# Regrouping the up-projection, splitting the last evictions and exchanges at the seams, and moving the second layer's filter loads, in a two-layer spectral and MLP kernel

## The chip, the cores and the metric

The kernel runs on one core of one Trainium2 chip. The metric is the device time of one execution in microseconds (us). The "span" of a profile is the time from the first to the last instruction of that one profiled execution, about 1.8 us less than the device time. Engines: PE is TensorE, PEld its weight loads, DVE is VectorE, ACT is ScalarE, POOL is GpSimd, SP is SyncE.

## The reference

```python
def _A_ref(x, w_r, w_i):                       # spectral filter
    X = jnp.fft.rfft2(x.astype(jnp.float32), axes=(-2, -1))
    return jnp.fft.irfft2(X * (w_r + 1j * w_i), s=(S, D), axes=(-2, -1)).astype(jnp.bfloat16)

def _B_ref(x, w1, b1, w2, b2):                 # MLP
    y = _layernorm(x)
    h = _gelu(jnp.einsum("bsd,df->bsf", y, w1) + b1)
    return jnp.einsum("bsf,fd->bsd", h, w2) + b2

# S, D, F = 2048, 576, 4608; twice:
x = x + _A_ref(_layernorm(x), A_w_r, A_w_i)
x = x + _B_ref(_layernorm(x), B_w1, B_b1, B_w2, B_b2)
```

## The kernel before

x stays on the chip as 16 tiles of 128 rows. Per layer the stages are:

1. The spectral-in stage folds, transposes and transforms each tile along D, and begins the transform along S. Each tile's result goes through an "exchange", a DMA that spreads it over other partitions. In layer 1 this stage is woven into the down-projection of layer 0, and only the last tile's part is left over at the layer boundary.
2. The middle stage finishes the forward transform, multiplies by the filter, begins the inverse, and exchanges again.
3. The spectral-out stage finishes the inverse and adds.
4. The MLP runs in four passes of four tiles. Each pass has an up-projection (36 chunks of 128 hidden units, in 18 pairs) and a down-projection.

D = 576 is four and a half times 128. The half remainder of a pair of chunks is done by two 64-row matmuls that run side by side in the two halves of the array (in the trace they start 0.003 to 0.004 us apart). In the code, `full` is the 128-row part of a pair and `rest` the 64-row part.

```python
# up-projection: groups of three pairs, each in one of three two-bank PSUM buffers
for p in range(0, NFC // 2, 3):
    for k in range(2):
        acc[p + k] = big_ps([P, 2, 512])
        full(p + k, True)                  # 8 matmuls of 128 rows
    acc[p + 2] = big_ps([P, 2, 512])
    for k in range(3):
        rest(p + k, k == 2)                # 2 matmuls of 64 rows each
    gelu(p)
    gelu(p + 1)
    full(p + 2, False)
    gelu(p + 2)
    ...

# layer boundary: the last tile's spectral-in work, with filler matmuls on zeros
spec.fold(prev, nc.vector)
keep_busy(5)
spec.turn(prev)                            # PE transposes, one ACT copy
keep_busy(4)
spec.sqrt = True
spec.stats([prev])
spec.dft_d(prev)                           # 6 matmuls, one scaled ACT eviction
keep_busy(5)
spec.dft_v(prev, on_act=True)              # 4 matmuls, one ACT copy, one exchange

# end of the middle stage
if n == NT - 1:
    nc.vector.tensor_copy(out=h[:, 0], in_=ph[:, 0, 0:KP])
    ins = nc.scalar.copy(out=h[:, 1], in_=ph[:, 1, 0:KP]).ins
...
exchange(hx, E_ORDER[n], h)                # then keep_busy(20) opens the next stage

# after the MLP of layer 0: filter and inverse-matrix loads of layer 1
for j in range(4):
    b = ("y1", order[-1]) if j >= 2 else None   # groups 2, 3 behind the last copy
    load_w(j, 0, b); load_w(j, 1, b); load_i1(j, b)
```

Of the kernel before, what the change touches and what calls it, by code (L numbers as in the profile page):

```python
# [18 lines left out]
P = 128  # L19
# [104 lines left out]
def kernel(  # L124
# [82 lines left out]
    nc.vector.memset(c_eps[:, 1:2], EPS * EPS)  # L207
    marks = {}

    def keep_busy(n):  # L210
        pw = sm_ps([P, 512], F32)
        for _ in range(n):
            nc.tensor.matmul(pw[:], lhsT=zeros[:], rhs=zeros[:, 0:1].to_broadcast([P, 512]), start=True, stop=True)  # L213
# [87 lines left out]
    class SpectralIn:  # L301
# [4 lines left out]
        def fold(self, t, odd_engine):  # L306
# [2 lines left out]
            odd_engine.tensor_tensor(out=xf[:, DH:D], in0=x_sb[:, t, 0:DH], in1=x_sb[:, t, DH:D], op=ALU.subtract)  # L309
            self.st["xf", t] = xf  # L310

        def stats(self, tiles):
            for t, (_, rs) in zip(tiles, ln_scale(ln_bn(tiles), False, self.sqrt)):
                self.st["rs", t] = rs

        def turn(self, t):
            xf = self.st.pop(("xf", t))
            pt = sm_ps([P, 5, P])
            for ci, (start, _) in enumerate(CHUNKS):
                nc.tensor.transpose(pt[:, ci, :], xf[:, start : start + 128], ident[:])  # L320
            xT = work.tile([P, 5, P], BF16, tag="turn")
            marks["turn", t] = nc.scalar.copy(out=xT[:], in_=pt[:]).ins
            self.st["xT", t] = xT

        def fold_twice(self, t):
# [19 lines left out]
            nc.sync.dma_start_transpose(out=xT[:], in_=rows[:])  # L345
            self.st["xT2", t] = xT

        def dft_d(self, t):
            pz = big_ps([P, 2, 512])
            if ("xT2", t) in self.st:  # L350
                xT = self.st.pop(("xT2", t))
                for o in range(2):
                    at_rest = 4 * KH + o * KP
                    nc.tensor.matmul(pz[:, o, 0:KP], lhsT=xT[:, 4, :], rhs=c_fd2[:, at_rest : at_rest + KP], start=True, stop=False)
                    for part in range(2):
                        g = FOLDS.index((o, part))
                        nc.tensor.matmul(  # L357
                            pz[:, o, part * KH : (part + 1) * KH], lhsT=xT[:, g, :], rhs=c_fd2[:, g * KH : (g + 1) * KH],
                            start=False, stop=(part == 1),
                        )  # L360
            else:
                xT = self.st.pop(("xT", t))
                for o in range(2):
                    for q, ci in enumerate(HALF_CHUNKS[o]):
                        nc.tensor.matmul(
                            pz[:, o, 0:KP], lhsT=xT[:, ci, :], rhs=c_fd[:, 3 * o + q, :], start=(q == 0), stop=(q == 2),
                        )
            z = work.tile([P, 2, KP], BF16, tag="z", bufs=3)
            nc.scalar.activation(  # L369
                out=z[:].rearrange("p r (j o) -> p r o j", o=2),  # L370
                in_=pz[:, :, 0:KP].rearrange("p o (r j) -> p r o j", r=2),
                func=ACT.Copy, scale=self.st.pop(("rs", t)),
            )
            self.st["z", t] = z

        def dft_v(self, t, on_act):
            z = self.st.pop(("z", t))
            py = big_ps([P, 2, 512])
            for r, terms in enumerate((((0, 0), (2, 1)), ((0, 1), (1, 0)))):
                for q, (pl, ri) in enumerate(terms):  # L380
                    nc.tensor.matmul(  # L381
                        py[:, r, 0:KP], lhsT=c_k1[:, pl, :], rhs=z[:, ri], start=(q == 0), stop=(q == 1)
                    )
            y1 = work.tile([P, 2, KP], BF16, tag="y1", bufs=5)
            if on_act:
                ins = nc.scalar.copy(out=y1[:], in_=py[:, :, 0:KP]).ins  # L386
            else:
                ins = nc.vector.tensor_copy(out=y1[:], in_=py[:, :, 0:KP]).ins
            marks["y1", t] = ins
            exchange(self.vx, t, y1[:])  # L390

        def run_all(self, loads):
# [6 lines left out]

            for i in range(NT + 4):  # L400
                if 0 <= i - 1 < NT:
                    self.turn(order[i - 1])
                if i < NT:
                    self.fold(order[i], nc.vector)
                    if i == 0:
                        moments(0)
                if i % 2 == 1 and i < NT:
                    for tt, (_, rs) in zip(order[i - 1 : i + 1], ln_scale(pairs.pop(i // 2), False, self.sqrt)):
                        self.st["rs", tt] = rs
                if 0 <= i - 4 < NT:  # L410
                    self.dft_v(order[i - 4], on_act=(i % 2 == 0))
                if 0 <= i - 2 < NT:
                    self.dft_d(order[i - 2])
                if i < 4:
                    keep_busy((5, 1, 1, 1)[i])
                if i + 1 < NT:
                    moments(i + 1)
                for call in loads.get(i, ()):
                    call()

    exchanged = {}

    def exchange(dst, slot, src):
        p0 = 32 * (slot // 4) + slot % 4
        ins = nc.sync.dma_start(out=dst[p0 : p0 + 29 : 4], in_=src).ins
        before = exchanged.setdefault(id(dst), [])
        for b in before:
            tc.declare_no_dep(ins, b, query=mybir.DependencyQuery.ANY_SYNC, reason="other partitions of the array")
# [2 lines left out]
    def middle(vx, hx, wks, i1s, loads):  # L431
# [32 lines left out]
        def idft_c(n):  # L464
# [5 lines left out]
                    nc.tensor.matmul(ph[:, o, 0:KP], lhsT=i1[:, n % 4, pl, :], rhs=xp[:, ri, :], start=(q == 0), stop=(q == 1))  # L470
            h = at(r_sb, [P, 2, KP], 592 * (2 + 9 + n % 8))
            if n == NT - 1:
                nc.vector.tensor_copy(out=h[:, 0], in_=ph[:, 0, 0:KP])
                ins = nc.scalar.copy(out=h[:, 1], in_=ph[:, 1, 0:KP]).ins
            elif n % 8 == 2:
                ins = nc.vector.tensor_copy(out=h[:], in_=ph[:, :, 0:KP]).ins
            else:
                ins = nc.scalar.copy(out=h[:], in_=ph[:, :, 0:KP]).ins
            marks["h", n] = ins
            exchange(hx, E_ORDER[n], h)  # L480

        keep_busy(12)
        for i in range(NT + 4):
# [173 lines left out]
    def mlp_up(yT, loads=()):  # L657
        hts = []
        loads = list(loads)
        acc = {}  # L660

        def full(p, first):
            ph = acc[p]
            for q in range(2):
                fc = 2 * p + q
                for ci in range(4):
                    nc.tensor.matmul(  # L667
                        ph[:, q, :], lhsT=w1_sb[:, ci, fc * 128 : (fc + 1) * 128], rhs=yT[:, ci, :],
                        start=(first and ci == 0), stop=(not first and ci == 3),
                    )  # L670

        def rest(p, first):
            for q in range(2):
                rows = slice(64 * q, 64 * q + 64)
                nc.tensor.matmul(acc[p][:, q, :], lhsT=w1r_sb[rows, p, :], rhs=yT[rows, 4, :], start=first, stop=not first)  # L675

        def gelu(p):
            for q in range(2):
                fc = 2 * p + q
                ht = at(h_sb, [P, 512], 512 * fc)  # L680
                marks["ht", fc] = nc.scalar.activation(  # L681
                    out=ht[:], in_=acc[p][:, q, :], func=ACT.Gelu_apprx_tanh, bias=b1_sb[:, fc : fc + 1], scale=1.0
                ).ins
                hts.append(ht)

        for p in range(0, NFC // 2, 3):
            for k in range(2):
                acc[p + k] = big_ps([P, 2, 512])
                full(p + k, True)
            acc[p + 2] = big_ps([P, 2, 512])  # L690
            for k in range(3):
                rest(p + k, k == 2)
            gelu(p)
            gelu(p + 1)
            full(p + 2, False)
            gelu(p + 2)
            if loads:
                loads.pop(0)(("ht", 2 * p))
        return hts
# [1 line left out]
    def mlp_down(t, i, hts, store, between):  # L701
# [3 lines left out]
        po = big_ps([P, 2, 512])  # L705

        def step(fc, h):
            nc.tensor.matmul(  # L708
                po[:, h, 0:DH], lhsT=hts[fc][:, i * 128 : (i + 1) * 128], rhs=w2_chunk(fc)[:, h * DH : (h + 1) * DH],
                start=(fc == 0), stop=(fc == NFC - 1),  # L710
            )

        if store and t == order[-1]:
            for h in range(2):
                for fc in range(NFC):
                    step(fc, h)
                nc.vector.tensor_tensor(out=xr[:, h], in0=po[:, h, 0:DH], in1=xb[:, h], op=ALU.add)  # L717
                nc.sync.dma_start(out=ov[:, t, h * DH : (h + 1) * DH], in_=xr[:, h])
            return
        for fc in range(NFC):  # L720
            for h in range(2):
# [8 lines left out]
    def mlp(li, prep, spec, loads):  # L730
        past = []
        last = li == N_LAYERS - 1
        for q in range(4):
# [6 lines left out]
            for i, t in enumerate(QUADS[q]):  # L740
# [17 lines left out]
                if spec is not None and len(past) > 1:  # L758
                    p = past[-2]
                    k = 2 if t != order[-1] else 0  # L760
                    slots[k].append(lambda p=p: spec.dft_d(p))
                    slots[k + 2].append(lambda p=p: spec.dft_v(p, on_act=True))
                mlp_down(t, i, hts, last, slots)
                past.append(t)
        if spec is not None:
            prev = past[-1]
            spec.fold(prev, nc.vector)
            keep_busy(5)
            spec.turn(prev)
            keep_busy(4)  # L770
            spec.sqrt = True
            spec.stats([prev])
            spec.dft_d(prev)
            keep_busy(5)
            spec.dft_v(prev, on_act=True)

    first = [("x", 2), ("x", 3)]
    for j in range(4):
# [13 lines left out]
    for li in range(N_LAYERS):  # L792
# [3 lines left out]
        if li == 0:  # L796
# [6 lines left out]
                6: [lambda b: load(c_fd2[:], const_ap("fd2"), b)],  # L803
                5: [lambda b: load(b2_bc[:], B_b2.partition_broadcast(P), b)],
            }
        middle(vx, hx, wks, i1s, mid_loads)
        if li == 0:
            b1p = sm_ps([P, NFC])
# [10 lines left out]
        else:  # L819
            vx, hx = at(b_sb, [P, 16, 2, KP]), at(v_sb, [P, 16, 2, KP])  # L820
            mlp(li, prep, SpectralIn(vx, sqrt=False), w2_loads)
            for j in range(4):
                b = ("y1", order[-1]) if j >= 2 else None
                load_w(j, 0, b)
                load_w(j, 1, b)
                load_i1(j, b)

_INS = ['A_x', 'A_w_r', 'A_w_i', 'B_x', 'B_w1', 'B_b1', 'B_w2', 'B_b2']
_OUTS = [((1, 2048, 576), 'bfloat16')]
# [24 lines left out]
```

## Time and profile before

The time before is 753.89 us, the median of 4 runs (753.38 to 754.26). Stage lengths below are start-to-start distances of matmuls in the profile of that kernel:

| stage | us | what limits it |
|---|---|---|
| spectral-in, layer 0 | 42.81 | varies from run to run |
| middle, layer 0 | 28.53 | the last 6.05 us are an exchange with fillers |
| spectral-out, each | 26.13 | |
| MLP, layer 0 | 300.92 | PE |
| boundary: last down-projection matmul to the middle stage | 9.32 | chain over all engines |
| middle, layer 1 | 27.10 | the last 4.61 us are an exchange with fillers |
| MLP, layer 1 | 286.66 | PE |

The first two lines of the profile page before give the span and the busy times. PE is busy 97% of the span:

```profile
span 752.0 us, 12318 instructions
PE 728.6 (97%) x5009; PEld 450.4 (60%) x5009; DVE 274.3 (36%) x930; ACT 312.6 (42%) x527; POOL 60.7 (8%) x110
```

The next lines are from the timeline of PE before, in an up-projection. The columns are start, length from the first start to the last end, engine, line, operation, output and inputs, shape and count; idle time before the group comes last in brackets, if there is any.

```profile
608.52 0.82 PE L675 MATMUL psb<-yT,w1r_sb 64*128 64x512 bf16 x6
609.28 5.35 PE L667 MATMUL psb<-yT,w_sb 128*128 128x512 bf16 x24
614.57 0.82 PE L675 MATMUL psb<-yT,w1r_sb 64*128 64x512 bf16 x6
```

There is no idle bracket: PE looks fully busy. Still, the period of 6.04 us (608.525 to 614.565 in the unrounded trace) is more than its matmuls need. Inside a run of equal matmuls, starts are 0.216 us apart. At the change from 128 to 64 rows the distance is 0.312, at the change back 0.311, and the next one is 0.226. That is 0.20 us more per group than 27 steps of 0.216. Modelled ends hide such a loss, so it has to be read from the starts.

At the layer boundary, PE before (L213 are the fillers, L320 the transposes, L365 and L381 the transforms, L440 the middle stage):

```profile
399.51 0.66 PE L381 MATMUL psb<-z,c_k 128*128 128x290 bf16 x4
400.01 1.25 PE L213 MATMUL pss<-zeros 128*128 128x512 bf16 x5
401.10 0.44 PE L320 MATMUL pss<-ident,xf 128*128 128x128 bf16 x5
401.37 1.03 PE L213 MATMUL pss<-zeros 128*128 128x512 bf16 x4
402.32 0.92 PE L365 MATMUL psb<-c_fd,xT 128*128 128x290 bf16 x6
403.08 1.25 PE L213 MATMUL pss<-zeros 128*128 128x512 bf16 x5
404.24 0.66 PE L381 MATMUL psb<-z,c_k 128*128 128x290 bf16 x4
404.74 2.77 PE L213 MATMUL pss<-zeros 128*128 128x512 bf16 x12
408.71 2.65 PE L440 MATMUL psb<-b_sb,c_f 128*128 128x290 bf16 x20 [1.20 <-DMA b_sb<-y]
```

Every group of fillers ends about where the useful group behind it begins. The data come in step with them: the fold that the transposes read ends at 401.03 us, the copy behind them at 402.26 and the scaled eviction at 404.19, each 0.05 to 0.07 us before the group that uses it starts. The fold waits for VectorE's add of the last tile, which is one instruction over the whole tile before:

```profile
399.71 0.76 DVE L726 TENSOR_TENSOR x_sb<-psb,xb 128x576 bf16<-128x576 f32 x1 [5.83 <-PE psb L708]
```

The ends of the two middle stages before, PE (L213 again are fillers, L508 the stage behind):

```profile
66.62 4.53 PE L213 MATMUL pss<-zeros 128*128 128x512 bf16 x20
72.33 0.60 PE L508 MATMUL pss<-c_r,b_sb 128*128 128x256 bf16 x4 [1.19 <-DMA b_sb<-shared]
...
431.33 4.52 PE L213 MATMUL pss<-zeros 128*128 128x512 bf16 x20
435.81 0.60 PE L508 MATMUL pss<-c_r,v_sb 128*128 128x256 bf16 x4
```

In layer 0 PE waits 1.19 us for the exchange after its fillers have run out; in layer 1 the fillers end last. The last tile of the kernel has one plain wait, of the second half on the add of the first:

```profile
744.32 2.12 PE L708 MATMUL psb<-v_sb,h_sb 128*128 128x288 bf16 x16 [0.55 <-DVE x_sb L717]
```

### The profile page before, as it was taken

To read this page: it belongs to the slowest core of one execution; us is meant where nothing else is said; L and a number is where in the kernel's file an instruction comes from. 1 tells how busy PE (TensorE), PEld (TensorE's weight loads), DVE (VectorE), ACT (ScalarE), POOL (GpSimd) and SP (SyncE) were. 2 spreads that over 40 slices of the span, in tenths; PEclk is the share of its full clock that TensorE was granted. 3 is DMA by queue.
4 is the path that set the end of the run, shared out by engine and by line. 5 is a ranking of instruction groups with operands and counts; after the bars stand their busy time and mean duration, and the time that the engine had idled before them with its cause. 6 is when DMAs were issued, how large, how long until landed. Compare 5 with 4: busy or idle time off the path is not lost. (4 is left out here: it accounts for less than half of the span.)

```text
span 752.0 us, 12318 instructions
## 1 busy us (share of the span) xinstructions
PE 728.6 (97%) x5009; PEld 450.4 (60%) x5009; DVE 274.3 (36%) x930; ACT 312.6 (42%) x527; POOL 60.7 (8%) x110
## 2 busy tenths in 40 slices
PE   7879999999999999999998998999999999999998
PEld 4645744784478447844785565457546744774476
DVE  6765970366036603630353969002400140010011
ACT  7955865114621453145323776530262035105600
POOL 3220002000100100000022000200100010000000
PEclk9999999999999999999999999999999999999999
DMA  7844926210121012110035400640002010100000
GB/s 247 232 140 146 280 81 229 54 44 26 44 56 49 26 45 53 51 35 0 18 85 177 123 21 16 218 120 17 34 17 44 17 42 2 44 17 9 1 17 17
DMA packets 49417, 54.45 MB, mean 72 GB/s; under 512 B 29892, under 2 KB 41104, under 8 KB 49360
## 3 DMA queue, kind: packets, MB, share of 16 engines
q0 software_dynamic: 7600, 29.10, 12.3%
q1 hardware_dynamic: 41328, 23.99, 12.0%
q8 instruction: 39, 0.64, 0.4%
q10 hardware_dynamic: 432, 0.58, 0.2%
q14 instruction: 18, 0.15, 0.1%
HBM read 29.34 MB, written 8.59 MB: 50 GB/s over the span
## 5 line engine op out<-in xcount | busy, mean ns | idle before, releaser
L681 ACT ACTIVATE h_sb<-psb,b_sb 128x512 bf16<-128x512 f32 x288 | 171.6, 695 | 231.2 <-PE psb L675 231.2
L708 PEld LDWEIGHTS <-h_sb 128*128 128x128 bf16 x2304 | 224.9, 98 | 58.3 <-issue 0.7
L667 PE MATMUL psb<-yT,w_sb 128*128 128x512 bf16 x1152 | 258.3, 379 | 0.1
L667 PEld LDWEIGHTS <-w_sb 128*128 128x128 bf16 x1152 | 108.7, 98 | 143.9 <-issue 20.6
L708 PE MATMUL psb<-shared,h_sb 128*128 128x288 bf16 x1280 | 166.8, 286 | 0.0
L726 DVE TENSOR_TENSOR x_sb<-psb,xb 128x576 bf16<-128x576 f32 x31 | 23.5, 757 | 356.8 <-PE psb L708 356.8
L708 PE MATMUL psb<-v_sb,h_sb 128*128 128x288 bf16 x1024 | 131.2, 286 | 0.5 <-DVE x_sb L717 0.5
L369 ACT ACTIVATE z<-psb,rs 128x580 bf16<-128x580 f32 x32 | 29.5, 920 | 89.9 <-PE psb L357 79.7
L273 DVE BATCH_NORM_STATS2 stats<-x_sb 128x6 f32<-128x288 bf16 x112 | 44.6, 440 | 1.1 <-DMA x_sb<-in_A_x_dram 1.1
L675 PE MATMUL psb<-yT,w1r_sb 64*128 64x512 bf16 x288 | 39.4, 380 | 0.0
L386 ACT CAST y<-psb 128x580 bf16<-128x580 f32 x24 | 15.5, 645 | 37.9 <-PE psb L381 36.7
L213 PE MATMUL pss<-zeros 128*128 128x512 bf16 x110 | 29.4, 396 | 1.0 <-DVE h_sb L229 1.0
L632 DVE TENSOR_SCALAR xn<-x_sb,mv,rs 128x576 bf16<-128x576 bf16 x24 | 9.3, 426 | 57.3 <-DMA quad<-xn 56.9
L544 DVE TENSOR_TENSOR shared<-psb,x_sb 128x576 f32<-128x576 f32 x32 | 24.0, 751 | 16.3 <-PE psb L536 16.2
L536 PE MATMUL psb<-c_gd,u 128*128 128x288 bf16 x128 | 24.9, 286 | 2.6 <-DVE x_sb L550 1.9
L442 ACT CAST shared<-psb 128x580 bf16<-128x580 f32 x32 | 20.4, 642 | 15.1 <-PE psb L440 10.5
L513 ACT CAST u<-pss 128x512 bf16<-128x512 f32 x32 | 18.6, 581 | 17.7 <-PE pss L508 17.1
L675 PEld LDWEIGHTS <-w1r_sb 64*128 64x128 bf16 x288 | 10.2, 94 | 26.0 <-issue 20.3
L470 PE MATMUL psb<-shared,h_sb 128*128 128x290 bf16 x128 | 21.4, 285 | 2.7 <-DVE shared L458 1.3
L704 DVE TENSOR_TENSOR xb<-x_sb,b_bc 128x576 f32<-128x576 bf16 x32 | 23.9, 748 | 0.0
L343 POOL DMA_DIRECT2D rows<-xf x14 | 7.6, 540 | 194.6 <-DVE xf L335 194.6
L381 PE MATMUL psb<-z,c_k 128*128 128x290 bf16 x128 | 21.1, 286 | 0.6 <-ACT z L369 0.6
(99 smaller groups left out, 521.3 us busy)
## 6 DMA issues: line engine op xcount, KB each, us to landing
shared<-in_B_w_dram POOLq DMA_DIRECT2D x4, 1440.0 KB, 7.8
w_sb<-in_B_w_dram SPq DMA_DIRECT2D x16, 288.0 KB
v_sb<-in_B_w_dram POOLq DMA_DIRECT2D x4, 1152.0 KB, 6.2
quad<-xn POOLq DMA_DIRECT2D x24, 160.0 KB, 2.6
h_sb<-const_i POOLq DMA_DIRECT2D x8, 384.0 KB, 6.1
v_sb<-y SPq DMA_DIRECT2D x16, 145.0 KB
b_sb<-shared SPq DMA_DIRECT2D x16, 145.0 KB
b_sb<-y SPq DMA_DIRECT2D x16, 145.0 KB
```

The source lines that it names most:

```text
L213: nc.tensor.matmul(pw[:], lhsT=zeros[:], rhs=zeros[:, 0:1].to_broadcast([P, 512]), start=True, stop=True)
L273: nc.vector.bn_stats(out=stats[:, h, :], in_=x_sb[:, t, h * DH : (h + 1) * DH])
L369: nc.scalar.activation(out=z[:].rearrange("p r (j o) -> p r o j", o=2), in_=pz[:, :, 0:KP].rearrange("p o (r j) -> p r o j", r=2), func=AC ...
L470: nc.tensor.matmul(ph[:, o, 0:KP], lhsT=i1[:, n % 4, pl, :], rhs=xp[:, ri, :], start=(q == 0), stop=(q == 1))
L536: nc.tensor.matmul(po[:, o, 0:DH], lhsT=lhsT, rhs=c_gd[:, 3 * o + q, :], start=(q == 0), stop=(q == 2))
L544: nc.vector.tensor_tensor(out=tt, in0=po[:, 0:1, 0:DH].to_broadcast([P, 2, DH]), in1=xr, op=ALU.add)
L667: nc.tensor.matmul(ph[:, q, :], lhsT=w1_sb[:, ci, fc * 128 : (fc + 1) * 128], rhs=yT[:, ci, :], start=(first and ci == 0), stop=(not first ...
L675: nc.tensor.matmul(acc[p][:, q, :], lhsT=w1r_sb[rows, p, :], rhs=yT[rows, 4, :], start=first, stop=not first)
L681: marks["ht", fc] = nc.scalar.activation(out=ht[:], in_=acc[p][:, q, :], func=ACT.Gelu_apprx_tanh, bias=b1_sb[:, fc : fc + 1], scale=1.0).ins
L704: nc.vector.tensor_tensor(out=xb[:], in0=xr, in1=b2_bc[:].rearrange("p (h n) -> p h n", h=2), op=ALU.add)
L708: nc.tensor.matmul(po[:, h, 0:DH], lhsT=hts[fc][:, i * 128 : (i + 1) * 128], rhs=w2_chunk(fc)[:, h * DH : (h + 1) * DH], start=(fc == 0), ...
L726: nc.vector.tensor_tensor(out=xr, in0=po[:, :, 0:DH], in1=xb[:], op=ALU.add)
```

## The change

The intent is to shorten what PE waits for or wastes at the seams. It has six parts:

- up-projection groups of four pairs instead of three, the fourth in the two one-bank PSUM buffers;
- both halves of the last tile's down-projection independent of each other, in both layers, each half with its own add, and at the layer boundary the layer norm's statistics by halves too;
- the last tile's evictions split over ScalarE and VectorE, with fewer fillers at the boundary (4, 3, 3 for 5, 4, 5);
- the last exchange of each spectral-in and middle stage in two halves;
- the two last copies of the middle stage side by side;
- the layer-1 loads of groups 2 and 3 moved into the middle stage.

```diff
+    def apart(a, b):
+        tc.declare_no_dep(b, a, query=mybir.DependencyQuery.ANY_SYNC, reason="other bank, other half of the tile")
...                                                    # turn, last tile
-            marks["turn", t] = nc.scalar.copy(out=xT[:], in_=pt[:]).ins
+            n = 3 if halved else 5
+            marks["turn", t] = nc.scalar.copy(out=xT[:, 0:n], in_=pt[:, 0:n]).ins
+            if halved:
+                nc.vector.tensor_copy(out=xT[:, n:5], in_=pt[:, n:5])
...                                                    # dft_d, last tile
+            if halved:
+                za = nc.scalar.activation(out=to[:, :, 0], in_=frm[:, :, 0], func=ACT.Copy, scale=rs).ins
+                apart(za, nc.vector.tensor_scalar(out=to[:, :, 1], in0=frm[:, :, 1], scalar1=rs, scalar2=None, op0=ALU.mult).ins)
...                                                    # dft_v, last tile
+            if halved:
+                for r in range(2):
+                    was, ins = ins if r else None, (nc.scalar.copy, nc.vector.tensor_copy)[r](out=y1[:, r], in_=py[:, r, 0:KP]).ins
+                    if r:
+                        apart(was, ins)
+                    exchange(self.vx, t, y1, r)
...                                                    # end of the middle stage
-                nc.vector.tensor_copy(out=h[:, 0], in_=ph[:, 0, 0:KP])
+                ha = nc.vector.tensor_copy(out=h[:, 0], in_=ph[:, 0, 0:KP]).ins
                 ins = nc.scalar.copy(out=h[:, 1], in_=ph[:, 1, 0:KP]).ins
+                apart(ha, ins)
...
-            exchange(hx, E_ORDER[n], h)
+            for r in (0, 1) if n == NT - 1 else (None,):
+                exchange(hx, E_ORDER[n], h, r)
...                                                    # mlp_up
-        for p in range(0, NFC // 2, 3): ...
+        for p in range(0, NFC // 2, 4):
+            ahead = [p, p + 1] if p + 3 < NFC // 2 else [p]
+            behind = [a + len(ahead) for a in ahead]
+            for a in ahead:
+                place(a)                               # p % 4 == 3: two small buffers
+                full(a, True)
+            for a in behind:
+                place(a)
+            for a in ahead + behind:
+                rest(a, a in behind)
+            for a in ahead:
+                gelu(a)
+            for a in behind:
+                full(a, False)
+                gelu(a)
...                                                    # mlp_down, last tile of each layer
+            for n in range(2 * NFC):
+                h, fc = divmod(n, NFC)
+                ins = step(fc, h).ins
+                if h == 1:
+                    apart(added, ins)
+                ...
...                                                    # layer boundary
-            keep_busy(5)
-            spec.turn(prev)
-            keep_busy(4)
-            spec.sqrt = True
-            spec.stats([prev])
-            spec.dft_d(prev)
-            keep_busy(5)
-            spec.dft_v(prev, on_act=True)
+            spec.stats_half(prev, 1)
+            spec.stats_end(prev)
+            keep_busy(4)
+            spec.turn(prev, halved=True)
+            spec.scale(prev)
+            keep_busy(3)
+            spec.dft_d(prev, halved=True)
+            keep_busy(3)
+            spec.dft_v(prev, on_act=True, halved=True)
...                                                    # loads of layer 1
+        if li == 1:
+            mid_loads = {
+                0: [lambda b: load_w(2, 0, b), lambda b: load_w(2, 1, b)],
+                1: [lambda b: load_i1(2, b), lambda b: load_w(3, 0, b)],
+                2: [lambda b: load_w(3, 1, b), lambda b: load_i1(3, b)],
+            }
...
-            for j in range(4):
-                b = ("y1", order[-1]) if j >= 2 else None
+            for j in range(2):
```

## The prediction

> What bounds the kernel now. TensorE is busy 97% of the 752 us span at full granted clock (busy table, slices). The two MLP stages take about 588 us of it (98 to 399, 462 to 749); the group table gives the 512-column up-projection matmuls 0.1 us of idle in all. So time can come only from (a) TensorE's pace in the up-projection and (b) the seams where TensorE waits or runs filler: end of the first spectral stage (41 to 44 us), of the first middle stage (67 to 72), the layer boundary (399 to 409), the end of the second middle stage (431 to 436), the last tile (744).
>
> Costs, term by term.
>
> 1. Up-projection grouping. The timeline repeats every 6.04 us: 24 full matmuls, 6 half-height ones. Full ones start 0.216 us apart, half-height pairs 0.216; at the change of height the distance is 0.312 going in, 0.311 coming out, plus 0.01 on the next: 0.20 us lost per group. The Trainium skill, "TensorEngine Tiling (Array Packing)", Key Properties, says a change of tiling mode drains the engine; the trace agrees. Groups per pass fall from 6 to 5, in 8 passes: -1.6 us. ScalarE needs about 1.2 us per pair of GELUs, TensorE 1.9, so the new PSUM placement should not stall; w2 loads are triggered later but land several us before use.
>
> 2. Last tile. TensorE waits between the halves for VectorE's add (chain of waits; it resumes at 744.32 instead of about 743.60). Removed: -0.7 us.
>
> 3. Layer boundary, all on the critical path. Before: last matmul starts 399.39, fillers hold the transposes until 401.10, copy 0.69, matmuls, scaled eviction 0.92, matmuls, copy 0.64, exchange issued 405.60, next stage starts 408.71. After: one filler fewer before the transposes (-0.22), eviction of 3 of 5 chunks (about -0.2; both engines read one bank, so I expect them one after the other, still covered by the first matmuls), scaled eviction on two engines (-0.4), last copy split (-0.2). The exchange becomes two issues; SyncE spends 0.71 us per issue back to back, so the second starts about 404.98: perhaps 0.1 more. Sum -1.1 us (0.7 to 1.4).
>
> 4. First spectral stage. The two last copies wait for exchanges of earlier tiles (buffer release, 1.2 and 1.8 us in the waits); DMA moves a steady 180 GB/s there. The halved work upstream hides behind that: -0.15 us.
>
> 5. Middle ends. The serial pair of copies (ScalarE waits 0.78 us for VectorE) becomes parallel, but in layer 0 the last exchange is bound by queue drain: -0.1. In layer 1 the 20 fillers end just when the next stage starts (435.81): 0.
>
> 6. Loads of layer 1. Two groups start about 4 us later, within the last tile, the others move into the middle stage. They should land 1 us before use; DMA there gets busier: +0.1, with a tail of +1.
>
> Sum: about -3.6 us, 750.3 us; 748.7 to 752.0 holds it 8 times in 10. Faster by over 2%: 1%; within 2%: 98%; slower by over 2%: 1%.
>
> What would show it. Half-height batches of 8 and 4, a pass 0.2 us shorter; no wait on the add at 744; boundary (last down-projection matmul to first of the middle stage) 8.2 us instead of 9.3; second middle stage unchanged, 27.1 us.
>
> What would make it wrong. Half exchanges of 580-byte packets landing later than one whole one; VectorE's half copy waiting for the first half exchange; layer-1 weights late, or their traffic delaying the last exchange as in layer 0 (4.8 us from issue to use there, 3.4 in layer 1); GELU stalls.

## The result

After: 751.22 us, the median of 11 runs (749.47 to 753.39). Before, in the same rounds and the earlier ones: 754.2 us, the median of 16 (752.29 to 759.3). The ratio is 0.9955 with a 95% interval of 0.9938 to 0.9973. It is not quite the ratio of those medians. The profiled execution of the kernel after has a span of 748.4 us, with PE again busy 97%. 0.9955 of 754.2 us is 3.4 us less, where 3.6 were predicted.

The stages, before and after. "Other profiles" are the runs below whose code in that stage equals the one named (the last row leaves out runs with a whole exchange, which moves the end; see below):

| stage | before | other profiles of that code | after | other profiles of that code | predicted change |
|---|---|---|---|---|---|
| spectral-in 0 | 42.81 | 41.84 to 43.86 | 42.85 | 42.00 to 44.23 | -0.15 |
| middle 0 | 28.53 | 27.79, 27.88, 28.03 | 27.40 | 27.39, 27.40, 27.81, 28.36, and 28.86 with half clock | -0.1 |
| MLP 0 | 300.92 | 300.92 | 300.08 | 300.09 | -0.8 |
| boundary | 9.32 | 9.34, 9.38, 9.43 | 8.49 | 8.47 to 8.50 | -1.1 |
| middle 1 | 27.10 | 27.04, 27.13, 27.26 | 27.57 | 27.37, 27.39, 27.49 | +0.1 |
| MLP 1 with last tile | 286.66 | 286.66 | 285.12 | 285.11, 285.12 | -1.5 |
| last matmul's start to the end | 3.42 | 3.41 to 3.43 | 3.67 | 3.66 to 3.68 | 0 |

The MLP, the boundary and the last tile repeat. Spectral-in and the first middle stage move by a microsecond or more between runs of one and the same code, which hides any small gain there.

The up-projection after, PE timeline (L708 are the 128-row and L716 the 64-row matmuls):

```profile
605.82 0.82 PE L716 MATMUL psb<-yT,w1r_sb 64*128 64x512 bf16 x6
606.48 0.38 PE L716 MATMUL pss<-yT,w1r_sb 64*128 64x512 bf16 x2
606.79 1.90 PE L708 MATMUL psb<-yT,w_sb 128*128 128x512 bf16 x8
```

The batch now has 8 matmuls of 64 rows. The cost of one change of height is as before: 605.506 to 605.817 going in (0.311), 606.476 to 606.787 coming out (0.311). There are fewer of them. The pass, start to start, is 71.31 us instead of 71.52.

The boundary after, PE (L216 fillers, L336 transposes, L384 and L403 transforms, L473 middle stage):

```profile
397.58 0.66 PE L403 MATMUL psb<-z,c_k 128*128 128x290 bf16 x4
398.08 1.03 PE L216 MATMUL pss<-zeros 128*128 128x512 bf16 x4
398.95 0.44 PE L336 MATMUL pss<-ident,xf 128*128 128x128 bf16 x5
399.23 0.81 PE L216 MATMUL pss<-zeros 128*128 128x512 bf16 x3
399.96 0.92 PE L384 MATMUL psb<-c_fd,xT 128*128 128x290 bf16 x6
400.72 0.81 PE L216 MATMUL pss<-zeros 128*128 128x512 bf16 x3
401.56 0.66 PE L403 MATMUL psb<-z,c_k 128*128 128x290 bf16 x4
402.05 2.77 PE L216 MATMUL pss<-zeros 128*128 128x512 bf16 x12
405.95 2.64 PE L473 MATMUL psb<-b_sb,c_f 128*128 128x290 bf16 x20 [1.12 <-DMA b_sb<-y]
```

Row by row against before: to the transposes 1.37 us instead of 1.59, from there to the first transform 1.01 for 1.22, to the second 1.60 for 1.92, to the middle stage 4.39 for 4.47. The last step holds the last copy, which is faster (0.46 us for 0.64), and the exchange, which is not (3.27 us from its first issue to its use, for 3.11). The first step holds an edit that is easy to overlook: only the second half's add is left at the seam, 0.46 us for 0.76.

```profile
397.79 0.46 DVE L765 TENSOR_TENSOR x_sb<-psb,xb 128x288 bf16<-128x288 f32 x1 [4.70 <-PE psb L753]
```

So the fold ends 0.30 us earlier, counted from the matmuls of the first row, and that is what let a filler go: with the old add the fold ended only 0.07 us before the transposes.

VectorE's part of the transposes' copy, after, in VectorE's timeline:

```profile
399.94 0.29 DVE L341 COPY xT<-pss 128x256 bf16<-128x256 bf16 x1 [0.52 <-ACT xT L339]
```

It waits for ScalarE's part, as the prediction expected. The Trainium skill, "PSUM — Partial Sum Buffer", section "PSUM bank collisions raise a hardware error", says that two engines must not access one PSUM bank on the same partitions at the same time, reads included; here both halves lie in one bank and the framework puts them one after the other (0.52 us of wait). It costs nothing, because the first transform's matmuls start on ScalarE's part.

The ends of the two middle stages after, PE (L543 is the stage behind):

```profile
66.66 4.53 PE L216 MATMUL pss<-zeros 128*128 128x512 bf16 x20
71.24 0.60 PE L543 MATMUL pss<-c_r,b_sb 128*128 128x256 bf16 x4
...
428.55 4.52 PE L216 MATMUL pss<-zeros 128*128 128x512 bf16 x20
433.52 0.60 PE L543 MATMUL pss<-c_r,v_sb 128*128 128x256 bf16 x4 [0.46 <-DMA v_sb<-shared]
```

The two have changed places in these two profiles: in layer 0 the wait for the exchange is gone, in layer 1 there is a new one of 0.46 us.

The last tile after, PE:

```profile
738.03 2.61 PE L753 MATMUL psb<-shared,h_sb 128*128 128x288 bf16 x20
740.48 2.12 PE L753 MATMUL psb<-v_sb,h_sb 128*128 128x288 bf16 x16
```

The second half follows without a gap. The 0.25 us lost at the very end comes from the closing checks. SyncE checks its DMA semaphores one after the other, 0.062 us each. Before, the last store's semaphore was late in the list and three checks remained after it; after, it is early in the list and seven remain. The change only renumbered the semaphores. Two runs below with one issue less, e6 and e8, agree: there the last store comes still later in the list, one check remains after it, and the end takes 3.31 and 3.30 us.

### The profile page after: what moved, and what is told of

It is laid out like the page before. It is cut to its first block, busy times and chain, and to the rows that moved or that the text cites. A ratio compares the mean times of both kernels' runs of the same rounds, so it can differ in the third digit from the quotient of the medians.

```text
span 748.4 us, 12355 instructions
## 1 busy us (share of the span) xinstructions
PE 726.5 (97%) x5005; PEld 451.5 (60%) x5005; DVE 276.3 (37%) x936; ACT 315.4 (42%) x528; POOL 60.6 (8%) x110
## 5 line engine op out<-in xcount | busy, mean ns | idle before, releaser
L722 ACT ACTIVATE h_sb<-psb,b_sb 128x512 bf16<-128x512 f32 x224 | 138.1, 686 | 225.8 <-PE psb L716 217.8
L708 PE MATMUL psb<-yT,w_sb 128*128 128x512 bf16 x896 | 206.9, 379 | 0.1
L708 PEld LDWEIGHTS <-w_sb 128*128 128x128 bf16 x1152 | 109.4, 98 | 142.4 <-issue 17.2
L395 ACT ACTIVATE z<-psb,rs 128x580 bf16<-128x580 f32 x30 | 27.6, 921 | 88.6 <-PE psb L376 79.8
L708 PE MATMUL pss<-yT,w_sb 128*128 128x512 bf16 x256 | 60.5, 379 | 0.0
L722 ACT ACTIVATE h_sb<-pss,b_sb 128x512 bf16<-128x512 f32 x64 | 40.5, 690 | 0.0
L716 PE MATMUL psb<-yT,w1r_sb 64*128 64x512 bf16 x224 | 31.1, 380 | 0.0
L216 PE MATMUL pss<-zeros 128*128 128x512 bf16 x106 | 28.4, 396 | 1.0 <-DVE h_sb L232 1.0
L716 PEld LDWEIGHTS <-w1r_sb 64*128 64x128 bf16 x288 | 10.8, 94 | 24.5 <-issue 17.0
```

The lines of the kernel that those rows point to most:

```text
L216: nc.tensor.matmul(pw[:], lhsT=zeros[:], rhs=zeros[:, 0:1].to_broadcast([P, 512]), start=True, stop=True)
L395: nc.scalar.activation(out=to, in_=frm, func=ACT.Copy, scale=rs)
L708: nc.tensor.matmul(acc[p][q], lhsT=w1_sb[:, ci, fc * 128 : (fc + 1) * 128], rhs=yT[:, ci, :], start=(first and ci == 0), stop=(not first a ...
L716: nc.tensor.matmul(acc[p][q], lhsT=w1r_sb[rows, p, :], rhs=yT[rows, 4, :], start=first, stop=not first)
L722: marks["ht", fc] = nc.scalar.activation(out=ht[:], in_=acc[p][q], func=ACT.Gelu_apprx_tanh, bias=b1_sb[:, fc : fc + 1], scale=1.0).ins
```

## The experiments

All twelve gave correct results. Theory: the time gained is (1) fewer changes of array height, (2) the removed wait in the last tile, (3) a shorter chain at the boundary, less what the exchanges and loads give back. The rivals are named with each run. Runs e3, e4, e6, e7, e8, e9 and e13 are single profiled executions (state unknown): their total times decide nothing, and only the stages of their profiles are used.

**Up-projection grouping alone (e1_group4).** The kernel before with the new `mlp_up`, nothing else.

```diff
-        for p in range(0, NFC // 2, 3):   # three pairs, big buffers
+        for p in range(0, NFC // 2, 4):   # four pairs, the fourth in the small buffers
```

> The kernel before with the up-projection grouping of the change alone (groups of four pairs, the fourth in the two small PSUM buffers). Theory (each change of array height costs about 0.20 us per group, 5 groups instead of 6): every pass from the second is 0.20 us shorter (71.52 to 71.32 in the second MLP), the whole 1.6 us shorter, seams as before. Rival (the gain in the MLP comes from the PSUM placement and earlier GELUs): then the start-to-start distances inside a group of full matmuls shrink or waits vanish, and the pass gain is not 0.20 us per group.

Measured: passes 71.31 for 71.52 us, MLP 300.09 and 285.82 for 300.92 and 286.66, so 1.67 us in eight passes. A run of 16 full matmuls takes 3.62 us in both. The time ratio, 0.9972 (0.9942 to 1.0002), is too wide to tell this alone.

**Groups of two pairs (e2_group2).** The same code made to change height more often.

```diff
-        for p in range(0, NFC // 2, 3):
+        for p in range(0, NFC // 2, 2):   # one pair ahead, one behind, big buffers only
```

> The kernel before with groups of two pairs, nine groups per pass instead of six, in the old PSUM buffers. Theory (height changes cost 0.20 us per group): each pass 3 x 0.20 = 0.60 us longer, the whole about 4.8 us longer. Rival (height changes are hidden or the cost is per half-height matmul): passes unchanged.

Measured: passes 72.15 us, so 0.63 more with three more groups, 0.21 per group. The MLPs took 303.45 and 289.18 us, together 5.05 more; time ratio 1.005 (1.0026 to 1.0074). PE in e2_group2:

```profile
609.13 0.60 PE L675 MATMUL psb<-yT,w1r_sb 64*128 64x512 bf16 x4
609.66 3.63 PE L667 MATMUL psb<-yT,w_sb 128*128 128x512 bf16 x16
613.22 0.60 PE L675 MATMUL psb<-yT,w1r_sb 64*128 64x512 bf16 x4
```

The period of 4.10 us (609.126 to 613.223) is 18 steps of 0.216 and 0.20 to 0.21 over. Raising the number of groups and cutting it give the same 0.21 us per group, with and without the new buffers. So it is the number of height changes, and not the PSUM placement. The Trainium skill, "TensorEngine Tiling (Array Packing)", "Key Properties", says that changing the tiling mode drains the engine, and gives no size; here in and out together cost 0.20 to 0.21 us.

**The kernel before, profiled again (e4_before_again).** No edit.

> The kernel before, unchanged, profiled a second time: how far the seams move by themselves. If the first middle stage again takes 28.5 us with 6.05 us from its last inverse matmul to the next stage, that long tail belongs to the kernel. If it takes 27.4 as in the kernel after, the 1.1 us gained there is a matter of chance and not of the change.

Measured: first middle stage 27.88 us, its tail 5.41. With e1 and e2, whose code there is the same, the old stage took 28.53, 27.88, 27.79 and 28.03 us. So nearly half of the 1.1 us between the two main profiles (28.53 against the old code's mean of 28.06) was chance on this side alone.

**The kernel after, profiled again (e3_after_again).** No edit.

> The kernel after, unchanged, profiled a second time. The MLP passes, the boundary (8.49 us) and the last tile should repeat within 0.1 us; the first spectral stage may move by a microsecond (41.8 to 43.9 in four profiles of the old stage). First middle stage: the old one took 28.53, 27.88, 27.79 and 28.03 us; if the change gains there, this is near 27.4 again; if chance, it lies in the old range.

Measured: MLPs and last tile within 0.01 us, boundary 8.50. First middle stage 27.81 us: its tail was 5.34 with a PE wait of 0.5 us on the exchange. The new stage thus also moves, but from a floor of 27.40, which is where the 20 fillers end.

**Old place of the layer-1 loads (e5_old_loads).**

```diff
-            for j in range(2):
-                load_w(j, 0); load_w(j, 1); load_i1(j)
+            for j in range(4):
+                b = ("y1", order[-1]) if j >= 2 else None
+                load_w(j, 0, b); load_w(j, 1, b); load_i1(j, b)
```

(and the loads within the middle stage taken out)

> The kernel after with the layer-1 loads put back to where they were before. Theory (the loads moved into the middle stage keep the DMA queue filled and delay the last exchange of layer 1): the second middle stage falls from 27.57 to about 27.1 us, the boundary grows by 0 to 0.3 us as the loads meet the last exchange. Rival (the split exchange is what delays it): it stays at 27.5 us.

Measured: boundary 10.30 us, 1.8 more, far beyond the 0 to 0.3 expected. The tail of the second middle stage fell from 5.10 to 4.64 as expected, but the stage got longer, 27.82 us, because of half clock at its start (below). The time ratio is 0.9984 (0.9956 to 1.0011): less gain than the change by its middle, but too wide to decide. PE in e5_old_loads, and the granted clock in windows of 2 us (columns: stretch, its length, busy time and count for PE, PEld, DVE, ACT, POOL, then granted clock, DMA share, GB/s):

```profile
407.53 3.96 PE L473 MATMUL psb<-b_sb,c_f 128*128 128x290 bf16 x20 [2.94 <-DMA b_sb<-y]
```

```profile
406.00:408.00 2.00, 0.47 (x3) 0.32 (x4) 0.00 (x0) 0.00 (x0) 1.48 (x2) 0.71 1.00 275
408.00:410.00 2.00, 2.00 (x10) 1.27 (x9) 0.63 (x2) 0.98 (x2) 0.00 (x0) 0.50 1.04 327
```

Two things happened. First, the packets of the exchange's second half came out between load packets, from 405.3 to 406.5 us, although SyncE had begun to issue it at 403.16; the first half had passed in 0.65 us (403.7 to 404.35). Second, PE stood still for 2.94 us, and 2.26 us into this pause, at 406.86 us, the clock dropped to half for 3.41 us: the 20 matmuls took 3.96 us instead of 2.64, and as long as the window lasted their starts are 0.241 us apart instead of 0.123. The Trainium skill, "TensorE: Matmul & The Clock Gate", "What's actually happening", describes a window of 3413 ns after which an idle array gets half its clock; the trace shows windows of exactly that length. So moving the loads was not the small cost that the prediction booked: with the split exchange it is what keeps the boundary at 8.5 us.

**Whole exchange in the middle stages (e6_whole_middle).**

```diff
-            for r in (0, 1) if n == NT - 1 else (None,):
+            for r in (None,):
```

> The kernel after with the last exchange of each middle stage whole instead of halved (the two copies still run side by side). If the halved exchange gives the gain at the end of the first middle stage, that stage goes from 27.4 back to about 28.0 us. If the gain comes from the copies side by side (0.4 us earlier), it stays at 27.4 to 27.6. If halving delays the landing (580-byte packets, a second issue 0.71 us later), both middle stages get 0.1 to 0.3 us shorter.

Measured: 27.40 and 27.39 us, against 27.40 or 27.81 and 27.57 or 27.37 with halves. Halving the exchange gains nothing here.

**Copies of the middle stage one after the other (e7_serial_middle).**

```diff
-                apart(ha, ins)
```

> The kernel after with the declared independence of the two last copies of the middle stage taken back, so that ScalarE waits for VectorE again (exchange still halved). If the copies side by side are what shortens the end of the first middle stage, the tail of both middle stages grows by about 0.3 us or more (first: 4.92 to 5.3 or more; second: 4.9 to 5.1 up to 5.3). If not, they stay, and the old 27.8 to 28.5 us are left unexplained.

Measured: 27.40 us again in the first middle stage, 27.54 in the second. So neither the copies side by side nor the halved exchange alone is needed for 27.40. Together with the fillers' floor this fits "either one suffices", but no run took both away from the kernel after, and the queue moves by chance. What shortened the first middle stage on average (from 28.06 us in the four profiles of the old code) stays open.

**Whole exchange at the boundary (e8_whole_y).** Copies still on two engines.

```diff
                 for r in range(2):
                     ...
-                    exchange(self.vx, t, y1, r)
                 marks["y1", t] = ins
+                exchange(self.vx, t, y1[:])
                 return
```

> The kernel after with the last exchange of the spectral stages whole (copies still split over two engines). One issue at about 402.72 instead of two at 402.69 and 403.40; an undisturbed whole exchange took 3.05 us from issue to use before. My sum then gives a boundary of 8.3 us, 0.2 shorter than with halves (8.49). Rival, the intent of the change: halves land earlier, and the boundary gets longer than 8.49.

Measured: boundary 8.17 us, 0.32 less than with halves. The trace of the kernel after shows why: the second half is issued 0.71 us behind the first (402.68 and 403.39), because SyncE spends that on one issue of an exchange, half or whole (whole ones issued back to back in the profile before are 0.71 to 0.72 us apart). The two halves' packets then move at 403.9 to 404.65 and 404.7 to 405.35 us. One whole issue can start as soon as both copies are done: counted from the last down-projection matmul, it starts at 5.32 us in e8, between the halves' 5.22 and 5.93 us.

**Earlier loads in the second middle stage (e9_early_loads).** Behind the twelfth filler, not behind the first products.

```diff
-        keep_busy(12)
+        marks["fill"] = keep_busy(12)
+        for call in loads.get(-1, ()):
+            call("fill")
...
-                0: [lambda b: load_w(2, 0, b), ...], 1: [...], 2: [...],
+                -1: [all six loads],
```

> The kernel after with the layer-1 loads of the last two groups released by the twelfth filler matmul of the second middle stage, about 5 us earlier than after (which waits for the first product of that stage), and about 2 us later than the loads that spoilt the boundary in the run with the old loads. Theory (the loads fill the DMA queue while exchanges run; in the old place they push the second half of the exchange back): boundary stays 8.49, and the tail of the second middle stage falls from 5.10 to about 4.6 us. If the halved exchange is to blame for the 5.10, it stays.

Measured: boundary 8.48 us, second middle stage 27.08 with a tail of 4.61. PE in e9_early_loads at the end of that stage:

```profile
431.40 4.51 PE L216 MATMUL pss<-zeros 128*128 128x512 bf16 x19
435.88 0.60 PE L546 MATMUL pss<-c_r,v_sb 128*128 128x256 bf16 x4
```

The wait for the exchange is gone (one filler's record is missing). So the 0.3 to 0.5 us lost in the second middle stage came from loads that ran late enough to collide with the exchanges, and not from the halves. The DMA records show how. Loads and exchanges go through different queues (POOL's and SyncE's), but they slow each other. In the profile after, the exchanges moved 34 to 53 packets of 1160 bytes per us while the loads ran (16 to 22 us behind the last down-projection matmul), and then had a backlog, 135 to 172 per us up to the last exchange, whose last packet ended at 35.18 us. In e9, where the loads were over by about 16 us, it ended at 34.87, although it was issued at the same time. This run is slow elsewhere: its first middle stage took 28.86 us, because the clock dropped at the end of a pause of 2.13 us:

```profile
45.23 4.29 PE L474 MATMUL psb<-v_sb,c_f 128*128 128x290 bf16 x20 [2.13 <-DMA v_sb<-y]
```

**Old numbers of fillers at the boundary (e13_old_fillers).** 5, 4, 5 for 4, 3, 3, the rest as after.

> The kernel after with the old numbers of fillers at the boundary (5, 4, 5 instead of 4, 3, 3). If fillers bound the boundary, the transposes start 0.22 us later and the second transform's matmuls another 0.2 to 0.4 later, so that the boundary grows from 8.49 to about 8.9 us. If data bound it, it stays at 8.5.

Measured: boundary 9.09 us, 0.60 more. PE in e13_old_fillers:

```profile
397.73 0.66 PE L403 MATMUL psb<-z,c_k 128*128 128x290 bf16 x4
...
399.31 0.44 PE L336 MATMUL pss<-ident,xf 128*128 128x128 bf16 x5
399.59 1.03 PE L216 MATMUL pss<-zeros 128*128 128x512 bf16 x4
400.46 0.91 PE L384 MATMUL psb<-c_fd,xT 128*128 128x290 bf16 x6
401.21 1.25 PE L216 MATMUL pss<-zeros 128*128 128x512 bf16 x5
402.30 0.66 PE L403 MATMUL psb<-z,c_k 128*128 128x290 bf16 x4
```

The steps are 1.58, 1.15 and 1.84 us, against 1.59, 1.22 and 1.92 before and 1.37, 1.01 and 1.60 after. Splitting the add and the evictions, with the fillers left alone, would have gained 0.16 us in these three steps. With the data as early as after, the fillers were on the critical path; with the old data (see the profile before) they ran out together. So most of the gain needed both edits; no run cut the fillers alone.

**A combination (e11_loads_whole).** As e9, with whole exchanges everywhere, and two layer-0 loads (a folding table and the output bias) moved from the middle stage to the MLP.

```diff
-                6: [lambda b: load(c_fd2[:], const_ap("fd2"), b)],
-                5: [lambda b: load(b2_bc[:], B_b2.partition_broadcast(P), b)],
...
+        if li == 0:
+            w2_loads[0] = lambda b: (load_w2(0, b), load(c_fd2[:], ...), load(b2_bc[:], ...))
```

> A combination meant to beat both: the kernel after, with the layer-1 loads released early (as in e9), two layer-0 loads (the second folding table and the broadcast output bias) moved from the first middle stage to the MLP, and all exchanges whole. From the stages of single profiles: boundary 8.17 us (whole exchange), second middle stage 27.1, first middle stage 27.4 or up to 0.3 less because its DMA queue is shorter at the end. About 1.0 us less than after, 0.5% less than before or more; the time of the first spectral stage will hide part of it.

Measured: 750.32 us (749.29 to 750.88, 4 runs), before on the same chip 754.0; ratio 0.9945 (0.9929 to 0.996). Boundary 8.15, second middle stage 26.97 us. In the first middle stage the tail stayed at 4.92, which is the fillers' floor, so the two layer-0 loads gained nothing that shows. The clock dropped there in this profile too, and the stage took 27.59 us.

**The same with more fillers ahead of the first middle stage (e12_bridge).**

```diff
-        marks["fill"] = keep_busy(12)
+        marks["fill"] = keep_busy(fill)       # 22 in layer 0, 12 in layer 1
```

> As e11, with 22 filler matmuls instead of 12 ahead of the first middle stage, so that TensorE does not stand still for 3 us there. In four of ten profiles the granted clock fell to half for one window of 3.41 us just behind or in that pause, and in one (e9) the first middle stage took 28.86 us instead of 27.4. Theory (the pause lets the clock drop): no such window near 40 to 46 us. Median 0.2 to 0.7 us below e11. Rival (the window comes whatever TensorE does there): windows remain; and if the fillers run on past the landing, the stage starts late by as much.

Measured: 748.98 us (748.11 to 751.11, 6 runs); ratio to before 0.9935 (0.9918 to 0.9952). This profile has no clock window between the start and the end, and the middle stage started at once behind the fillers:

```profile
39.31 4.73 PE L216 MATMUL pss<-zeros 128*128 128x512 bf16 x21
43.93 2.64 PE L474 MATMUL psb<-v_sb,c_f 128*128 128x290 bf16 x20
```

One profile can't show that the window never comes: with 12 fillers it came near 40 to 46 us in 5 of 13 profiles. But the traces say when it comes. Within a profile all changes of clock lie whole multiples of 3.413 us apart. Cut into such windows from 15 us to the end, the fourteen profiles hold six in which PE was idle for 2.05 to 2.27 us, and half clock followed each of them; after none of the other 3,000 or so, with at most 1.84 us idle, did it follow. What counts is thus how much of a pause falls into one window. In e9 the whole 2.13 us lay in the window from 41.82 to 45.23 us, and the clock dropped; in e7 a pause of 2.13 us fell across a border at 43.14 us, 1.41 us in one window and 0.72 in the next, and it did not. In e12 no window there has more than 0.9 us idle. The stage sums put e12 about 1 us below the kernel after (boundary 8.14 for 8.49, second middle stage 26.97 for 27.57, end 3.43 for 3.67), and its interval lies below that of before. Against the kernel after, the intervals of the ratios overlap, and the two were not timed in the same rounds; so e12 beats before clearly, and after by its stages and its median.

## Why the prediction was right or wrong

The total was right: 750.3 us predicted, 751.2 measured, within 748.7 to 752.0. Several terms were not, and their errors cancelled.

The nearness to the 3.6 us is in part luck: the two main profiles differ by 3.58 us, but 1.13 us of that is the first middle stage, mostly chance, where 0.1 was predicted.

1. Grouping, -1.6 predicted: right. 1.67 us in e1, and 0.21 us per group in both directions.
2. Last tile, -0.7 predicted: right. MLP 1 lost 1.54 us, of which four passes make 0.82 to 0.84 (e1), so 0.70 to 0.72 remain. MLP 0 lost 0.84, which is the grouping alone: in layer 0 the independent halves gave nothing inside the stage, and what they gave lies at the boundary.
3. Boundary, -1.1 (0.7 to 1.4) predicted: 0.83 to 0.94 measured. The steps of "one filler fewer before the transposes (-0.22)" and "eviction of 3 of 5 chunks (about -0.2)" came out at 0.22 and 0.21, that of "scaled eviction on two engines (-0.4)" at 0.32. The wrong step was "perhaps 0.1 more" for the two issues: halving costs 0.32 us (e8). The prediction had the 0.71 us per issue and still gave it the wrong sign. It also named one filler where all the removed ones count: 0.60 us of the gain goes back with the old numbers (e13). And it did not name the add by halves, without which that one filler had at most 0.07 us to give.
4. Spectral-in, -0.15: not decided. The stage moves by 2 us between runs of one code.
5. "In layer 0 the last exchange is bound by queue drain: -0.1": mis-sized. The four profiles of the old code average 28.06 us, the five of the new code at full clock (27.39, 27.40, 27.40, 27.81, 28.36) 27.67. That is a gain of 0.4 us with a larger spread, down to a floor set by the fillers; which edit made it is open.
6. "The others move into the middle stage ... +0.1": the wrong account. Late loads cost 0.3 to 0.5 us at the end of the second middle stage (e9 gets it back). But the old place would have cost 1.8 us at the boundary, once the exchange is in two halves and the loads of the first groups come later (e5). "Second middle stage unchanged, 27.1 us" was wrong for the same reason: 27.4 to 27.6. The prediction listed this danger among what would make it wrong, and priced it too low.
7. Not foreseen: 0.25 us at the end, from the order of the closing semaphore checks.

## What to carry to other kernels

Count the changes of tiling mode on TensorE, not the small matmuls: each pair of changes costs the same whether the batch between them is short or long, and the busy figure doesn't show it, but start-to-start distances do. When a chain is shortened at a seam, the filler matmuls in it must be cut as well, or they keep the old pace; where a pause remains, enough of them must stay to keep the clock up. Splitting a small DMA into two issues pays only if the second half can be issued and landed earlier than the whole would have been; and loads that move at the same time belong well before or well after it, even when they have a queue of their own.

## What the Trainium skill lacked or had wrong

- "TensorEngine Tiling (Array Packing)", "Key Properties", names the drain at a change of tiling mode without a size. Here 128 to 64 rows and back cost 0.20 to 0.21 us per pair of changes, whatever the length of the batch (4, 6 or 8 matmuls of 512 columns).
- "TensorE: Matmul & The Clock Gate", "HAM oscillation — how this bites in real kernels", gives the rule to avoid idle gaps above about 3.4 us. Here the clock dropped to half for a window of 3.41 us at or behind pauses of 2.13 us (e9) and 2.26 us (e11) and inside one of 2.94 us (e5), while a pause of 2.98 us in the profile before brought no drop. What separates them is the idle time within one window of 3.413 us: 2.05 us or more in all six windows that half clock followed, at most 1.84 us in all others. Whether a pause of 2 to 3 us does harm is chance as far as its place among the windows is.
- No page that I read says what the semaphore checks at the end of a kernel cost: 0.062 us each here, one after the other, so that the place of the last store's semaphore in the list moved the end by 0.25 us.
